# An attention and experts kernel: moving the splits off GpSimd and the second head's copies to ScalarE, with float64 words converted in blocks of 512

## The chip, the cores and the metric

The kernel runs on one core of a Trainium2 chip. The metric is the device time of one execution in microseconds. Before the change the median of three runs is 1041.32 us (1040.53 to 1044.79).

## What is computed

Attention over 4 batches, 8 heads, 576 positions and 64 values per head, with a bias that a small network makes of the distance of two positions; then a dense feed-forward (2304 tokens, 512 to 2048 to 512); then a routed one, in which each token goes to one of 8 experts. Cut to what matters:

```
scores = q @ k.T / sqrt(D) + bias
attn   = softmax(scores, axis=-1)
x = (attn @ v).reshape(2304, 512)
h = x @ w_in                          # w_in, w_out come as float64
x = maximum(0.01 * h, h) @ w_out
expert = argmax(normalised x @ normalised expert_emb / tau)
out[t] = gate[t] * (maximum(x[t] @ w1[expert], 0) @ w2[expert])
```

## The kernel before

**Splits.** The matmuls with weights and keys run on numbers in two parts: a high part (a rounded copy, type fp32r) and a low part (the exact value less the high part). So each operand that is split costs a copy (a line of the table `COPY`) and a subtraction (`LO`). Letters say which engine does them: P is GpSimd (POOL in the profile), A is ScalarE (ACT), D is VectorE (DVE). A string of four letters has one letter per batch, or for `WIN_*` one per four of the 16 column blocks of `w_in`. The helpers stand at L70 (ScalarE's copy), L74 (GpSimd's), L78 (VectorE's), L82 and L86 (the subtractions).

**float64 words.** `w_in` and `w_out` arrive as pairs of 32-bit words. `convert_f64` (L93) makes float32 of them with three VectorE operations (L99, L102, L105), of 256 elements per partition each. `w_in_split` (L120) loads half a column block of `w_in` (256 KB, L124), converts it and splits it into two resident tiles. `w_out_narrow` (L694) loads half a row block of `w_out` (L698), converts it and stores the float32 to DRAM (L703); it is read back only after attention. There are 32 of each. Raw words and results have two buffers each.

**Attention.** `phase1` (L559) walks 80 steps: 4 batches, in each two parts of the query rows (`hf`), four pairs of heads (`p`) and two or three blocks of rows (`ib`). A step has two heads, except where `ib` is 4: there both heads, 64 rows each, share one piece. In a step PE transposes the probabilities (L460, L482), the result is copied from PSUM to SBUF by the engine that `PROB_T` names (L464, L466), PE makes the scores two steps ahead (L409), VectorE adds the bias and takes the row's extreme (L414), ScalarE takes the exponential (L422), and `normalise` (L427) multiplies by the reciprocal sum, head by head, on the engine that `NORM` names. After a group PE multiplies by the values (L496). Between these pieces the program hands in 12-matmul pieces of `x @ w_in` for the groups that are done (`up_units`, L509); ScalarE, later ScalarE and then VectorE, empty their PSUM buffers (L527, L528, L530), of which there are two.

**What sets the order.** Side jobs (loads, splits, conversions) are put at a step and one of two positions in it (`put`, L577). The program is written in that order, but a scheduler then orders each engine's instructions by its own model, and may draw a job forward when its engine is idle there. On the chip each engine, and each queue of DMA issues, runs its list strictly in order. Nearly all loads are issued by the queue SP: the bias tiles of each step (L383 to L388), q, k, v, the raw words, and the stores of the converted words.

**After attention** come the rest of `x @ w_in`, the product with `w_out` (L769), and the experts (L1257, L1288). They hold little that the change touches.

Of the kernel before, what the change touches and what calls it, by code (L numbers as in the profile page):

```python
# [7 lines left out]
F32 = mybir.dt.float32  # L8
# [4 lines left out]
U32 = mybir.dt.uint32  # L13
# [34 lines left out]
NORM = ("PDDD", "PADD")  # L50
# [38 lines left out]
COPY = {"P": copy_pool, "A": copy_act, "D": copy_dve}  # L89
# [3 lines left out]
def convert_f64(nc, raw, t):  # L93


    w = raw.rearrange("p k (n two) -> p k n two", two=2)
    lo, hi = w[:, :, :, 0], w[:, :, :, 1]
    tu = t.bitcast(U32)
    nc.vector.tensor_scalar(  # L99
        out=tu, in0=hi, scalar1=3, scalar2=0x3FFFFFF8, op0=ALU.logical_shift_left, op1=ALU.bitwise_and  # L100
    )
    nc.vector.scalar_tensor_tensor(  # L102
        out=tu, in0=hi, scalar=0xC0000000, in1=tu, op0=ALU.bitwise_and, op1=ALU.bitwise_or
    )
    nc.vector.scalar_tensor_tensor(  # L105
        out=tu, in0=lo, scalar=29, in1=tu, op0=ALU.logical_shift_right, op1=ALU.bitwise_or
    )


def w_in_columns(e, f):  # L110

    c = 128 * (f % (KF // 2))
    return [w[:, :, c:c + 128] for w in e.wi[f // (KF // 2)]]
# [3 lines left out]
    return [p.tile([128, KD, FF // 2], F32R, name=f"wi{k}") for k in range(2)]  # L117


def w_in_split(nc, e, f, half):  # L120

    raw = e.cv.tile([128, 2, 256], U32, tag="w_raw", name="w_raw", bufs=2)
    src = e.w_in.rearrange("(k p) n -> p k n", p=128)
    nc.sync.dma_start(out=raw, in_=src[:, 2 * half:2 * half + 2, 256 * f:256 * f + 256])  # L124
    kc = slice(2 * half, 2 * half + 2)
    hi, lo = (w[:, kc] for w in w_in_columns(e, f))
    t = e.cv.tile([128, 2, 128], F32, tag="w_t", name="w_t", bufs=2)
    convert_f64(nc, raw, t)
# [155 lines left out]
class Attention:  # L284
# [142 lines left out]
    def normalise(self, st):  # L427
# [24 lines left out]
    def transposes(self, st, h):  # L452
        nc, e = self.nc, self.e
        b, hf, p, ib = st
        pr, _ = self.prob[st]
        ph, _ = self.pt
        o = 128 * (ib - HALVES[hf][2][0])
        ps = e.psT.tile([128, 512], F32, tag="t", name="pst")
        for c in range(4):
            nc.tensor.transpose(ps[:, 128 * c:128 * c + 128], pr[:, h, 64 * h + 128 * c:][:, :128], e.ident)  # L460
        if ib == 4:
            src = ps.rearrange("p (c h i) -> p h c i", c=4, h=2)
            for hh in range(2):
                COPY[PROB_T[b]](nc, ph[:, hh, :, o:o + 64], src[:, hh])  # L464
        else:
            COPY[PROB_T[b]](nc, ph[:, h, :, o:o + 128], ps.rearrange("p (c i) -> p c i", c=4))  # L466

    def transpose_tail(self, st):

        nc, e = self.nc, self.e  # L470
        b, hf, p, ib = st
        pr, _ = self.prob[st]
        pt = self.pt[1]
        o = 128 * (ib - HALVES[hf][2][0])
        ps = e.psT.tile([128, 512], F32, tag="t", name="psx")
# [83 lines left out]
def phase1(ctx, tc, e):  # L559

    nc = tc.nc
# [15 lines left out]
    def put(n, pos, f, *args):  # L577
        todo.setdefault((max(n, 0), pos), []).append((f, args))
# [5 lines left out]
    for k, g in enumerate(groups):  # L584
        b, hf, p = g
# [14 lines left out]
    for k in range(2 * KF):  # L600
        put(3 + k // 2 if k < KF else 12 + (k - KF) // 2, k % 2, w_in_split, nc, e, k // 2, k % 2)
    for k in range(2 * KF):
        put(20 + k, k % 2, w_out_narrow, nc, e, k // 2, k % 2)
# [750 lines left out]
def program(tc, e):  # L1354
# [4 lines left out]
    with ExitStack() as top:  # L1359
# [82 lines left out]
```

## Time and profile before

| | us |
|---|---|
| median of three runs | 1041.32 |
| the profiled execution, its own time | 1044.42 |
| its span in the trace | 1042.6 |
| PE busy | 991.1 (95%) |
| VectorE busy | 735.9 (71%) |
| ScalarE busy | 467.7 (45%) |
| GpSimd busy | 164.0 (16%) |

The span is the stretch from the first to the last instruction in the trace; some 1.8 us lie around it. Busy shares are means over the whole kernel, of which attention is the first half; what each engine does in a stage is read from a table by stretches. Ends of matmuls are modelled in this profile, so that PE busy is not PE at its peak; the weight loads (PEld) are a second reading of the same engine.

### The profile page before, as it was taken

What the parts mean: (1) busy time and instruction counts of PE and PEld (TensorE: products, weight loads), DVE (VectorE), ACT (ScalarE), POOL (GpSimd) and SP (SyncE); (2) the same over time, 40 slices, a digit from 0 to 9 for tenths busy, and PEclk for the clock granted to TensorE, in tenths of its full rate; (3) what the DMA queues carried; (4) which work ended last, traced back from release to release, by engine and by line L of the source; (5) the groups of instructions that cost most, each with busy time, mean ns of one, the idle gap of its engine ahead of it and who ended that gap; (6) DMA issues with size and microseconds to landing.
All of it is one profiled execution on the core that took longest, in us unless ns stands there. A gap on an engine that the chain in (4) does not pass through costs nothing.

```text
span 1042.6 us, 19336 instructions
## 1 busy us (share of the span) xinstructions
PE 991.1 (95%) x6294; PEld 809.0 (78%) x6294; DVE 735.9 (71%) x1907; ACT 467.7 (45%) x950; POOL 164.0 (16%) x204
## 2 busy tenths in 40 slices
PE   5999988999989999999999999999999999999995
PEld 2455777888778988898888888888877888888884
DVE  8878999888989899778866666769984256313312
ACT  5778665443333333333344333345462355424422
POOL 3233465000201011110000000001002111111210
PEclk9999999999999999999999999999999999999998
DMA  7877788877678576545357534336605158313410
GB/s 224 238 230 217 236 270 267 269 225 218 209 238 277 153 209 203 168 138 147 113 182 221 191 112 121 111 112 216 178 21 212 42 180 281 129 41 99 152 41 22
DMA packets 142466, 180.17 MB, mean 173 GB/s; under 512 B 20609, under 2 KB 94721, under 8 KB 142226
## 3 DMA queue, kind: packets, MB, share of 16 engines
q1 hardware_dynamic: 120418, 149.31, 47.0%
q10 hardware_dynamic: 18576, 19.03, 5.2%
q0 software_dynamic: 3360, 10.49, 3.0%
q8 instruction: 52, 0.85, 0.3%
q14 instruction: 60, 0.49, 0.2%
HBM read 196.18 MB, written 43.94 MB: 230 GB/s over the span
## 4 chain that ended last, share of the span: by engine, by line
PE 68%; DVE 16%; DMA 8%; issue 5%; ACT 1%; POOL 1%; SPq 0%; DVEq 0%; ACTq 0%; POOLq 0%
PE psx L769 19%; PE pu L1257 10%; PE pd L1288 10%; PE psh L521 9%; PE psv L496 5%; PE pss L409 4%; PE psb L266 4%; PE pst L460 4%; DMA wo_raw<-in_w_out_dram 3%; DVE prob L414 2%; DMA w_raw<-in_w_in_dram 2%; DVE kt L82 2%; DVE pth L78 2%; PE pt L1268 2%; DVE prob L438 1%
## 5 line engine op out<-in xcount | busy, mean ns | idle before, releaser
L521 PE MATMUL psh<-x,wi 128*128 128x256 f32 (+1 forms) x1536 | 229.5, 299 | 5.6 <-DVE hst L528 3.1
L521 PEld LDWEIGHTS psh<-x,wi 128*128 128x128 f32 x1536 | 212.5, 190 | 9.0 <-DVE hst L528 4.7
L422 ACT ACTIVATE prob<-prob,stat 128x576 f32<-128x576 f32 x144 | 111.6, 775 | 177.4 <-DVE stat L414 157.3
L769 PE MATMUL psx<-woh,gh 128*128 128x512 f32 x288 | 113.0, 392 | 0.1
L769 PE MATMUL psx<-wol,gh 128*128 128x512 f32 x288 | 112.7, 391 | 0.0
L769 PE MATMUL psx<-woh,gl 128*128 128x512 f32 x288 | 112.2, 390 | 0.0
L414 DVE CUSTOM_DVE_ANT_0 prob<-pss,prob 128x576 f32<-128x576 f32 x144 | 107.8, 750 | 4.4 <-PE pss L409 2.6
L460 PE MATMUL pst<-ident,prob 128*128 128x128 f32 x576 | 90.7, 279 | 9.1 <-DVE pth L78 4.0
L70 ACT ACTIVATE gh<-g 128x512 fp32r<-128x512 f32 x72 | 45.4, 632 | 115.7 <-PE psx L769 104.5
L460 PEld LDWEIGHTS pst<-ident,prob 128*128 128x128 f32 x576 | 66.0, 140 | 30.2 <-issue 12.0
L78 DVE COPY pth<-pst 128x512 f32<-128x512 f32 (+1 forms) x120 | 74.7, 632 | 12.2 <-PE pst L460 11.7
L409 PE MATMUL pss<-kt,qhi 128*128 128x288 f32 x256 | 81.2, 332 | 1.1 <-DVE stat L414 1.1
L496 PE MATMUL psv<-pth,vs 128*64 128x256 f32 (+1 forms) x512 | 73.3, 413 | 1.7 <-DVE pth L78 1.6
L266 PE MATMUL psb<-mk,cf 128*32 128x79 f32 (+47 forms) x640 | 61.0, 411 | 13.9 <-POOL cf L250 6.9
L409 PE MATMUL pss<-kt,qlo 128*128 128x288 f32 x256 | 72.7, 299 | 0.0
L1288 PE MATMUL pd<-w2h,hth 128*128 128x512 f32 x160 | 67.9, 424 | 4.1 <-ACTq L1213 4.1
L786 DVE SCALAR_TENSOR_TENSOR junk<-x1s,en 128x512 bf16<-128x512 f32 x96 | 66.1, 689 | 3.0 <-DMA en<-en_d 1.9
L82 DVE TENSOR_TENSOR htl<-pt,hth 128x512 fp32r<-128x512 f32 x40 | 27.1, 690 | 57.8 <-ACT hth L70 57.8
L82 DVE TENSOR_TENSOR gl<-g,gh 128x512 fp32r<-128x512 f32 x72 | 49.4, 689 | 23.6 <-ACT gh L70 19.3
L82 DVE TENSOR_TENSOR xl<-pt,xh 128x512 fp32r<-128x512 f32 x21 | 14.4, 690 | 72.4 <-ACT xh L70 72.4
L1257 PE MATMUL pu<-w1h,xh 128*128 128x512 f32 x160 | 65.1, 407 | 0.3 <-ACT xh L70 0.3
L1288 PE MATMUL pd<-w2h,htl 128*128 128x512 f32 x160 | 64.6, 404 | 0.0
(229 smaller groups left out, 1911.6 us busy)
## 6 DMA issues: line engine op xcount, KB each, us to landing
ws<-in_mw_dram SPq DMA_DIRECT2D x164, 512.0 KB
prob<-bias SPq DMA_DIRECT2D x64, 288.0 KB
g<-h SPq DMA_DIRECT2D x72, 256.0 KB
prob<-bias SPq DMA_DIRECT2D x64, 256.0 KB
bias<-bt SPq DMA_DIRECT2D x36, 295.5 KB
h<-hst ACTq DMA_DIRECT2D x64, 160.0 KB
w_raw<-in_w_in_dram SPq DMA_DIRECT2D x32, 256.0 KB
h<-hst ACTq DMA_DIRECT2D x64, 128.0 KB
```

What stands on the lines that cost most here:

```text
L78: nc.vector.tensor_copy(out, in_)
L82: nc.vector.tensor_tensor(out=out, in0=x, in1=hi.bitcast(F32), op=ALU.subtract)
L266: nc.tensor.matmul(ps[32 * q:32 * q + 32, :b - a], lhsT=cf[:, 4 * (m % COEF_M) + q], rhs=x, start=True, stop=True, tile_position=(0, 32 * q),)
L409: nc.tensor.matmul(ps[:, jh, :288], lhsT=lhsT, rhs=kt[:, c0 + 288 * jh:][:, :288], start=(k == 0), stop=(k == len(ops) - 1),)
L414: nc.vector.tensor_tensor_reduce(out=prv, in0=ps[:, :, :288], in1=prv, scale=-0.125, scalar=3.0e38, op0=ALU.add, op1=ALU.min, accum_out=st ...
L422: nc.scalar.activation(out=pr[:, h], in_=pr[:, h], func=AF.Exp, bias=stat[:, 0, h:h + 1], scale=-1.0, accum_out=stat[:, 1, h:h + 1],)
L460: nc.tensor.transpose(ps[:, 128 * c:128 * c + 128], pr[:, h, 64 * h + 128 * c:][:, :128], e.ident)
L496: nc.tensor.matmul(ps[64 * h:64 * h + 64, :n], lhsT=vs[:, c, h], rhs=ph[:, h, c, :n] if c < 4 else pt[:, :n], start=(c == 0), stop=(c == 4 ...
L521: nc.tensor.matmul(ps[:, :n], lhsT=w[:, kc], rhs=x[:, kc, :n], start=(k == 0), stop=(k == 3 * KD - 1),)
L769: nc.tensor.matmul(ps, lhsT=a[:, c % 4], rhs=w[:, c], start=(k == 0), stop=(k == 3 * KF - 1))
L1257: nc.tensor.matmul(ps, lhsT=a[:, k], rhs=w[:, k, c], start=(i == 0), stop=(i == 3 * KD - 1))
L1288: nc.tensor.matmul(ps, lhsT=a[:, k], rhs=w[:, k], start=(k == 0 and j == 0), stop=(k == 7 and j == 2))
```

## The change

The tables give GpSimd's splits to other engines: of `w_in` (high parts of the later half to ScalarE, the rest to VectorE), of q (high to ScalarE, low to VectorE), and keys of batches 2 and 3 go from VectorE to ScalarE. `NORM` for the second head in batches 2 and 3, and `PROB_T` for the second head in batches 1 to 3, go from VectorE to ScalarE. GpSimd keeps the key copies and the normalisations of batch 0, and the first small products of the bias. `convert_f64` works on 512 elements at a time, 16 blocks each of `w_in` and `w_out`, and the load, the three operations and the split of a block are handed in at successive half steps by the new `spread`.

```
-WIN_HI, WIN_LO = "DPPP", "DDPP"
-K_HI, K_LO = "PADD", "DDDD"
-Q_HI, Q_LO = "APPP", "DDPP"
-PROB_T = "ADDD"
+WIN_HI, WIN_LO = "DDAA", "DDDD"
+K_HI, K_LO = "PAAA", "DDDD"
+Q_HI, Q_LO = "AAAA", "DDDD"
+PROB_T = ("ADDD", "AAAA")
-NORM = ("PDDD", "PADD")
+NORM = ("PDDD", "PAAA")
...
-    raw = e.cv.tile([128, 2, 256], U32, tag="w_raw", name="w_raw", bufs=2)
+    raw = e.cv.tile([128, KD * 256], U32, tag="w_raw", name="w_raw", bufs=2)
...
+    yield
+    t = e.cv.tile([128, KD * 128], F32, tag="w_t", name="w_t", bufs=2)
+    yield from convert_f64(nc, raw, t)
...
-                COPY[PROB_T[b]](nc, ph[:, hh, :, o:o + 64], src[:, hh])
+                COPY[PROB_T[hh][b]](nc, ph[:, hh, :, o:o + 64], src[:, hh])
...
+    def spread_on(k, it, gap):
+        try:
+            next(it)
+        except StopIteration:
+            return
+        put((k + gap) // 2, (k + gap) % 2, spread_on, k + gap, it, gap)
+
+    for f in range(KF):
+        spread(2 + f if f < KF // 2 else 3 + f, 0, lambda f=f: w_in_split(nc, e, f), 1)
+    for c in range(KF):
+        spread(20 + 2 * c, 0, lambda c=c: w_out_narrow(nc, e, c), 1)
...
-    raw = e.cv.tile([128, 2, 256], U32, tag="w_raw", name="wo_raw", bufs=2)
+    raw = e.cv.tile([128, 2 * DM], U32, tag="w_raw", name="wo_raw", bufs=2)
     r = slice(128 * c, 128 * c + 128)
-    nc.sync.dma_start(
-        out=raw, in_=e.w_out[r, 512 * half:512 * half + 512].rearrange("p (k n) -> p k n", k=2)
-    )
+    nc.sync.dma_start(out=raw, in_=e.w_out[r])
```

**The order on VectorE.** The order of PE's matmuls against each other stays, but the conversions move on VectorE: of `w_out`, the last operation stood behind the 88th of the 144 score operations (L414, `ISA prob,stat`), and now stands behind the 64th (36 belong to each batch). All 16 blocks now lie in batch 1; the program text would put them in batches 1 and 2. From the 53rd score operation, before (`pst` is the transposes' PSUM buffer, `pth` where they are copied):

```order
L414 ISA prob,stat<-pss,prob 128x576
L414 ISA stat 128x1
L99 TENSOR_SCALAR wo_t<-wo_raw 128x256
L102 SCALAR_TENSOR_TENSOR wo_t<-wo_raw,wo_t 128x256
L99 TENSOR_SCALAR wo_t<-wo_raw 128x256
L105 SCALAR_TENSOR_TENSOR wo_t<-wo_raw,wo_t 128x256
L78 COPY pth<-pst 128x4x128
```

And now, from the same operation:

```order
L418 ISA prob,stat<-pss,prob 128x576
L418 ISA stat 128x1
L442 TENSOR_SCALAR prob<-prob,stat 128x576
L107 SCALAR_TENSOR_TENSOR wo_t<-wo_raw,wo_t 128x512
L99 TENSOR_SCALAR wo_t<-wo_raw 128x512
L418 ISA prob,stat<-pss,prob 128x576
L418 ISA stat 128x1
L103 SCALAR_TENSOR_TENSOR wo_t<-wo_raw,wo_t 128x512
```

A block now is as large as two before, and blocks follow each other about as closely as the halves did.

**The order on the queue SP.** The loads move with them: before, the 32 loads of `w_out` halves stood between the bias loads of steps 25 and 50; now 16 loads of 512 KB stand between those of steps 23 and 36. The loads around the bias tile of one step in batch 1 (`bias` is the DRAM tensor, `prob` the tile it is loaded to), before:

```order
L703 DMA wo<-wo_t 128x256 x2
L698 DMA wo_raw<-in_w_out_dram 128x512 x2
L385 DMA prob<-bias_63 128x576
L387 DMA prob<-bias_63 128x512
L388 DMA prob<-bias_63 128x64
```

And now, around the bias tile of a like step:

```order
L714 DMA wo_raw<-in_w_out_dram 128x1024
L389 DMA prob<-bias_63 128x576
L391 DMA prob<-bias_63 128x512
L392 DMA prob<-bias_63 128x64
L718 DMA wo<-wo_t 128x512
L714 DMA wo_raw<-in_w_out_dram 128x1024
L718 DMA wo<-wo_t 128x512
L714 DMA wo_raw<-in_w_out_dram 128x1024
```

A store (L718) waits for VectorE's last operation on its block, and the bias loads behind it wait with it.

**The order on ScalarE.** In batch 2, from the 93rd of the 144 exponentials, before:

```order
L422 ACTIVATE prob,stat<-prob,stat 128x576
L70 ACTIVATE hst<-psh 128x320
L531 DMA h<-hst 128x320
L70 ACTIVATE hst<-psh 128x256
L422 ACTIVATE prob,stat<-prob,stat 128x576
L531 DMA h<-hst 128x256
```

And now, where `kt` waits for a key load, `pth` for PE's transposes, and `hst` frees a PSUM buffer for PE:

```order
L426 ACTIVATE prob,stat<-prob,stat 128x576
L70 ACTIVATE kt<-kraw 64x576
L70 ACTIVATE hst<-psh 128x320
L535 DMA h<-hst 128x320
L426 ACTIVATE prob,stat<-prob,stat 128x576
L70 ACTIVATE hst<-psh 128x256
L70 ACTIVATE pth<-pst 128x4x128
L535 DMA h<-hst 128x256
L70 ACTIVATE qhi<-qraw 128x512
```

Behind each exponential there now stand two to four instructions where one or two stood.

## Rows read from the trace of the kernel before

**Rows 1.** Busy time by stretches: the start, late batch 0, batches 1, 2 and 3.
```profile
core 0: us, PE busy (x) PEld busy (x) DVE busy (x) ACT busy (x) POOL busy (x), PEclk, DMA share, GB/s
0.00:100.00 100.00, 85.92 (x792) 41.50 (x793) 84.98 (x214) 73.00 (x156) 31.41 (x47) 1.00 0.77 229
100.00:165.00 65.00, 58.15 (x454) 47.92 (x455) 58.27 (x161) 42.49 (x105) 36.79 (x51) 1.00 0.81 247
165.00:294.00 129.00, 117.94 (x877) 102.69 (x877) 112.72 (x317) 56.74 (x130) 17.65 (x28) 1.00 0.78 241
294.00:413.00 119.00, 116.47 (x883) 103.43 (x883) 107.31 (x290) 41.88 (x105) 17.56 (x20) 0.99 0.70 211
413.00:528.00 115.00, 115.00 (x894) 103.38 (x893) 94.98 (x267) 42.13 (x106) 13.03 (x16) 1.00 0.45 137
```

**Rows 2.** Exponentials of batch 1 by the same table; each counts twice, with its accumulator read.
```profile
165.00:294.00 129.00, 31.37 (x73) 1.00 0.78 241
```

**Rows 3.** The same table for the stretch after attention up to the experts.
```profile
575.00:780.00 205.00, 204.03 (x950) 167.65 (x948) 156.08 (x452) 85.36 (x151) 3.03 (x2) 1.00 0.44 134
```

**Rows 4.** VectorE by shape, batch 1: line, count, busy us, mean ns, idle before, releaser.
```profile
L78 DVE COPY pth<-pst 128x512 f32<-128x512 f32 x31 | 21.1, 684 | 1.0 <-PE pst L460 0.9
L438 DVE TENSOR_SCALAR prob<-prob,stat 128x576 f32<-128x576 f32 x20 | 10.6, 528 | 0.3
L102 DVE SCALAR_TENSOR_TENSOR wo_t<-wo_raw,wo_t 128x256 uint32<-128x256 uint32 x20 | 8.1, 420 | 0.1
L99 DVE TENSOR_SCALAR wo_t<-wo_raw 128x256 uint32<-128x256 uint32 x20 | 6.5, 330 | 7.7 <-DMA wo_raw<-in_w_out_dram 7.5
L82 DVE TENSOR_TENSOR qlo<-qraw,qhi 128x512 fp32r<-128x512 f32 x7 | 4.8, 687 | 3.6 <-POOL qhi L74 3.6
...
L78 DVE CAST kt<-kraw 64x576 fp32r<-64x576 f32 x7 | 3.2, 452 | 0.5 <-DMA kraw<-in_k_dram 0.4
...
L78 DVE COPY pth<-pst 128x256 f32<-128x256 f32 x6 | 2.3, 418 | 0.0
```

**Rows 5.** VectorE's waits in batch 3: us in total, times, longest.
```profile
DVE pth L78 <- PE pst L460: 7.7, 11, 1.0
DVE hst L528 <- ACT hst L527: 5.2, 9, 1.5
```

**Rows 6.** VectorE by shape, all of attention: the conversions and splits of `w_in`.
```profile
L102 DVE SCALAR_TENSOR_TENSOR w_t<-w_raw,w_t 128x256 uint32<-128x256 uint32 x32 | 16.3, 510 | 0.2
L105 DVE SCALAR_TENSOR_TENSOR w_t<-w_raw,w_t 128x256 uint32<-128x256 uint32 x32 | 16.0, 500 | 0.3
...
L99 DVE TENSOR_SCALAR w_t<-w_raw 128x256 uint32<-128x256 uint32 x32 | 12.1, 378 | 2.9 <-DMA w_raw<-in_w_in_dram 2.6
...
L82 DVE TENSOR_TENSOR wi<-w_t,wi 128x256 fp32r<-128x256 f32 x16 | 7.2, 448 | 1.0 <-POOL wi L74 0.8
...
L78 DVE CAST wi<-w_t 128x256 fp32r<-128x256 f32 x8 | 2.7, 336 | 0.0
```

**Rows 7.** The page's groups: a three-operand VectorE operation of 512 elements, after attention.
```profile
L786 DVE SCALAR_TENSOR_TENSOR junk<-x1s,en 128x512 bf16<-128x512 f32 x96 | 66.1, 689 | 3.0 <-DMA en<-en_d 1.9
```

**Rows 8.** VectorE by shape, 0 to 130 us: a one-operand operation of 512 elements.
```profile
L220 DVE TENSOR_SCALAR mk<-lw,v 128x512 f32<-128x512 f32 x5 | 3.0, 640 | 0.0
```

**Rows 9.** Busy time by stretches of 10 us, the columns of rows 1: where DMA is busiest.
```profile
195.00:205.00 10.00, 10.00 (x79) 9.21 (x79) 9.71 (x32) 6.90 (x15) 1.09 (x2) 1.00 0.90 287
325.00:335.00 10.00, 9.50 (x69) 7.88 (x68) 9.93 (x26) 2.94 (x9) 2.00 (x2) 1.00 0.95 289
```

**Rows 10.** ScalarE by shape, 60 to 330 us.
```profile
L70 ACT ACTIVATE pth<-pst 128x512 f32<-128x512 f32 x29 | 17.2, 592 | 9.1 <-PE pst L460 6.5 <-PE psv L496 1.6 <-ACT hst L70 0.5
...
L436 ACT ACTIVATE prob<-prob,stat 128x576 f32<-128x576 f32 x16 | 12.3, 770 | 6.5 <-DVE stat L432 6.5
...
L70 ACT ACTIVATE kt<-kraw 64x576 fp32r<-64x576 f32 x8 | 5.5, 682 | 2.1 <-DMA kraw<-in_k_dram 2.0
...
L70 ACT ACTIVATE qhi<-qraw 128x512 fp32r<-128x512 f32 x5 | 3.1, 625 | 0.0
```

More of the change, by code (lines that the diff above doesn't have):

```diff
@@ L93, in convert_f64 @@
 def convert_f64(nc, raw, t):
-    w = raw.rearrange("p k (n two) -> p k n two", two=2)
-    lo, hi = w[:, :, :, 0], w[:, :, :, 1]
+    w = raw.rearrange("p (n two) -> p n two", two=2)
+    lo, hi = w[:, :, 0], w[:, :, 1]
     tu = t.bitcast(U32)
@@ L104, in convert_f64 @@
     )
+    yield
     nc.vector.scalar_tensor_tensor(
@@ L117, in new_w_in, with w_in_split @@
     return [p.tile([128, KD, FF // 2], F32R, name=f"wi{k}") for k in range(2)]
-def w_in_split(nc, e, f, half):
-    raw = e.cv.tile([128, 2, 256], U32, tag="w_raw", name="w_raw", bufs=2)
+def w_in_split(nc, e, f):
+    raw = e.cv.tile([128, KD * 256], U32, tag="w_raw", name="w_raw", bufs=2)
     src = e.w_in.rearrange("(k p) n -> p k n", p=128)
[L124 to L128, printed above, removed]
+    nc.sync.dma_start(out=raw.rearrange("p (k n) -> p k n", k=KD), in_=src[:, :, 256 * f:256 * f + 256])
+    yield
+    t = e.cv.tile([128, KD * 128], F32, tag="w_t", name="w_t", bufs=2)
+    yield from convert_f64(nc, raw, t)
+    yield
+    hi, lo = w_in_columns(e, f)
+    t = t.rearrange("p (k n) -> p k n", k=KD)
     COPY[WIN_HI[f // 4]](nc, hi, t)
@@ L463, in transposes @@
             for hh in range(2):
-                COPY[PROB_T[b]](nc, ph[:, hh, :, o:o + 64], src[:, hh])
+                COPY[PROB_T[hh][b]](nc, ph[:, hh, :, o:o + 64], src[:, hh])
         else:
-            COPY[PROB_T[b]](nc, ph[:, h, :, o:o + 128], ps.rearrange("p (c i) -> p c i", c=4))
+            COPY[PROB_T[h][b]](nc, ph[:, h, :, o:o + 128], ps.rearrange("p (c i) -> p c i", c=4))
     def transpose_tail(self, st):
@@ L475, in transpose_tail @@
         ps = e.psT.tile([128, 512], F32, tag="t", name="psx")
-        copy = COPY[PROB_T[b]]
+        copy = COPY[PROB_T[0][b]]
         if ib == 4:
@@ L598, in phase1, with spread @@
             put(m + 3, 1, at.v_load, b, p)
[L600 to L603, printed above, removed]
+    def spread(n, pos, job, gap):
+        k = 2 * n + pos
+        put(k // 2, k % 2, lambda: spread_on(k, iter(job()), gap))
+    def spread_on(k, it, gap):
[8 more added lines that the diff above has]
+        spread(20 + 2 * c, 0, lambda c=c: w_out_narrow(nc, e, c), 1)
     bias_setup(nc, e)
@@ L691, in phase1, with w_out_narrow @@
     return fl
-def w_out_narrow(nc, e, c, half):
-    raw = e.cv.tile([128, 2, 256], U32, tag="w_raw", name="wo_raw", bufs=2)
+def w_out_narrow(nc, e, c):
+    raw = e.cv.tile([128, 2 * DM], U32, tag="w_raw", name="wo_raw", bufs=2)
     r = slice(128 * c, 128 * c + 128)
-    nc.sync.dma_start(
-        out=raw, in_=e.w_out[r, 512 * half:512 * half + 512].rearrange("p (k n) -> p k n", k=2)
-    )
-    t = e.cv.tile([128, 2, 128], F32, tag="w_t", name="wo_t", bufs=2)
-    convert_f64(nc, raw, t)
-    nc.sync.dma_start(out=e.wo_d[r, 256 * half:256 * half + 256], in_=t.rearrange("p k n -> p (k n)"))
+    nc.sync.dma_start(out=raw, in_=e.w_out[r])
+    yield
+    t = e.cv.tile([128, DM], F32, tag="w_t", name="wo_t", bufs=2)
+    yield from convert_f64(nc, raw, t)
+    nc.sync.dma_start(out=e.wo_d[r], in_=t)
 def w_out_units(nc, e):
```

## The prediction

> **What bounds the kernel now.** I read the table by stretches first, then each engine's instructions by shape, then the waits. Each batch of attention has 36 exponentials: the count in [rows 2], which has each twice, bears out that 165 to 294 us is batch 1, and the stretches beside it batches 2 and 3. The reader is to see in [rows 1] that the three batches hold the same PE work (103 us of weight loads in each), yet take 129, 119 and 115 us. What differs is VectorE: 112.7, 107.3 and 95.0 us busy. In batch 3 PE's row shows no gap in 115 us, and it is VectorE that waits for PE, 7.7 us for transposes [rows 5]. So **batch 3 goes at PE's pace, batches 1 and 2 at VectorE's**; late batch 0 also has VectorE at 58.3 of 65 us. DMA is the third: 0.78 to 0.81 of its engines' time in batches 0 and 1, 0.45 in batch 3. ScalarE has room: 56.7 of 129, 41.9 of 119, 42.1 of 115. Behind attention PE is full [rows 3] and the change touches nothing there that PE waits for; I count 0.
>
> **Batch 3: what leaves VectorE.** Second-head copies: 16 of 512 elements at 684 ns and 4 of 256 at 418 [rows 4], 12.6 us. Second-head normalisations: 16 at 528 ns, 8.5 us. Key copies: 8 at 452 ns, 3.6 us. What comes: 8 low parts of q at 687 ns, 5.5 us. Net 19.2 us off, 95 to 76. ScalarE gets [rows 10] 16 x 0.592, 4 x about 0.38 (my estimate, between the 592 ns of 512 elements and nothing), 16 x 0.770, 8 x 0.682 and 8 x 0.625 us: 33.8 us, 42 to 76 of 115. Since PE already sets the pace, I take 0.5 us of gain; the work that hides the rest is PE's own.
>
> **Batch 2.** The same 19.2 us, and the 12 halves of `w_out` that are converted here now (32 less 20 in [rows 4]) go to batch 1: each costs 0.330 + 2 x 0.420 = 1.17 us, 14 us together. VectorE 107.3 to 74. It then goes at PE's pace, as batch 3: 119 to 115.5, **3.5 us gained**. The cover that is lost is VectorE's own; late next is PE.
>
> **Batch 1.** Off: the copies, 12.6 us. The `w_out` work: 20 halves at 1.17 us, 23.4 us, become 16 blocks of 512 elements. A two-operand operation on those is priced by [rows 7], 689 ns. The one-operand one is not in the trace at 512 elements: between 0.33 [rows 4] and 0.64 us [rows 8], which reads a scalar beside; I take 0.43, nearer to the first, as the half has the same operands. A block is then 1.81 us, 16 are 29.0: 5.6 us more. By VectorE's new order the last three blocks of `w_in` fall here too: 3 x (1.81 + 0.69 for the low part) against some 6 halves at 1.39 now [rows 6], about 0. Net 7 us off: 112.7 to 105.7. VectorE's idle time, 16.3 us, loses the 3.6 us for GpSimd's high parts of q [rows 4], as ScalarE has room; the 7.5 us for `w_out` loads I leave, since the blocks follow as closely as the halves did. That makes 105.7 + 12.7 = 118.4 us by VectorE.
>
> But the loads that come forward must fit. DMA works 0.78 x 129 = 100.6 us here, at 241/0.78 = 309 GB/s. Twelve halves more, each 256 KB in and 128 KB out, are 4.7 MB, 15.3 us: 115.9 us of DMA work. The busiest ten microseconds show a share of 0.90 and 0.95 [rows 9]. At 0.95 batch 1 takes 122, at 0.90, 129. I take 123, near the first, since the new loads are large and prefetched by two blocks: **6 us gained**. The SP queue is the place: a store waits for VectorE, and the next bias tile waits behind the store.
>
> **Batch 0 and the start.** VectorE's `w_in` work: 32 x (0.378 + 0.510 + 0.500) = 44.4 us [rows 6] becomes 16 x 1.81 = 29.0, 15.4 us less. It takes on 8 low parts (5.5 us) and 4 high parts of GpSimd (1.7); larger pieces save 1.7 on the low parts it had (16 x 0.448 against 8 x 0.69) and 1.0 on the high ones (8 x 0.336 against 4 x 0.43). Net 10.9 us, of which 2 were counted in batch 1: 9 us off 143.3 busy in 165. The ends are 0, if DMA (0.81) or the bias's small products on GpSimd hold the pace, and 9, if VectorE does throughout. I take **4 us**, the middle, since late batch 0 has VectorE at 0.90 and DMA at 0.81.
>
> Two prices of one kind bear on this: with GpSimd busy 68 of 165 us, an operation that takes 420 ns on `w_out` takes 510 on `w_in` [rows 4, 6]. That is in the 44.4, and I count it gone.
>
> **The sum.** 4 + 6 + 3.5 + 0.5 = 14 us. The profiled execution took 1044.4 us, so 1030.4; the median of the runs lies 3.1 below it, so **1027.3 us** for the median after.
>
> **A rule against the change.** The rows give ScalarE 592 ns for a 512-element copy out of PSUM and VectorE 684, but for a normalisation from SBUF 770 against 528. The Trainium skill, in "ScalarE: Activation LUTs", section Rules for kernel authors, says to use VectorE and not ScalarE for multiplications and the like. By that rule the 32 normalisations of batches 2 and 3 lose 32 x 0.242 = 7.7 us of engine time, and were ScalarE the bound the sum would be 6.3 and not 14. The trace agrees on the price, but with ScalarE at 42 of 115 us the lost time lies beside PE's; and on the copies out of PSUM it says the opposite.
>
> **The rivals.**
>
> *PE is not full in batch 3.* The ends of matmuls are modelled, and weight loads fill 103.4 of 115 us, 0.90. If PE has gaps that VectorE's late copies cause, a relieved VectorE closes half of them: batches 2 and 3 go to 109 us, 10 and 6 gained in place of 3.5 and 0.5, the sum 26: **1015 us**. For it: VectorE is at 95 of 115 there, and copies of 0.68 us stand between PE's transposes and its products. Against: in the trace PE waits for nothing in batch 3. The skill's "Perfetto Trace Analysis", section Identifying the Most-Contended Engine, calls matmul busy time a bad measure and the weight loads' share a good one; by that rule this rival holds. The rows between agree in part: after attention weight loads show 167.7 of 205 us, 0.82, with PE without a gap [rows 3], so a share of 0.90 need not mean room. Chance 0.20.
>
> *The drawn-forward `w_out` loads eat the gain.* DMA in batch 1 holds no more than 0.88: 115.9 / 0.88 = 132 us, 3 lost; late batch 0 gains 3, not 4. Sum 3 - 3 + 3.5 + 0.5 = 4: **1037 us**, no change that shows. For it: `wo_raw` loads already stop VectorE for 7.5 us in batch 1, and a block takes longer to land than a half. Against: they are half as many, and steps 37 to 51 are free of them. Chance 0.18.
>
> *ScalarE's queue holds PE up: slower.* In batches 2 and 3 a normalisation waits for VectorE's reciprocal and a key copy for its load, and behind them in the same queue stand the instructions that empty PE's two PSUM buffers. If each of the 32 normalisations costs PE its whole 0.77 us, 24.6 us are lost: 14 - 24.6 = 10.6 us slower, **1052 us**. It decides from 14/32 = 0.44 us each. For it: in batch 3 VectorE already waits 5.2 us for ScalarE's part of emptying them [rows 5], and ScalarE goes from 42 to 76 us. Against: that is still two thirds, and the second head's turn comes half a step after the first's. Chance 0.14.
>
> **How the numbers follow.** The forecast has 0.48. A measurement of this kernel tells about 0.5%, 5.2 us, from no change. Faster by more: the forecast and the first rival, 0.68. Within it: the second, 0.18. Slower: the third, 0.14. The range takes in the bounds: below, 0 to 165 at its full 9, batch 1 at VectorE's 118.4 (10.6) and the first rival's 16 are 36 us together, 1006, which needs all at once; I stop at 1012. Above it reaches past the second rival to 1043, and leaves out most of the third.
>
> **What would show it.** Right: batch 2 at 114 to 117 us with VectorE near 75 and PE without gaps; batch 1 at 120 to 126 with DMA near 0.93; batch 3 at 114 or 115; no waits for GpSimd's q. Wrong: batch 3 under 112 (the first rival); `wo_raw` waits on VectorE above 15 us or batch 1 above 128 (the second); weight loads of PE waiting on `hst` or `pth` of ScalarE, batch 3 above 118 (the third); or a change in the stretch after attention, which I hold for untouched.

## The result, and the profile after

The changed kernel's median is **1028.76 us** (1027.66 to 1030.66, four runs), against 1041.46 (1040.53 to 1044.79, four runs) of the kernel before on the same chip: a ratio of 0.9881, with a 95% interval of 0.9855 to 0.9907. The forecast was 1027.3. The profiled execution took 1027.66 us, with a span of 1025.9; GpSimd's 61 us less and ScalarE's 80 more show on its page:

```profile
span 1025.9 us, 19107 instructions
PE 985.7 (96%) x6294; PEld 809.2 (79%) x6294; DVE 682.8 (67%) x1719; ACT 547.8 (53%) x1102; POOL 103.0 (10%) x112
```

The table by stretches of the changed kernel, with the columns of [rows 1]: late batch 0, batches 1, 2 and 3, and the stretch after attention.

```profile
107.00:161.00 54.00, 50.13 (x387) 42.30 (x386) 51.73 (x124) 41.16 (x103) 19.72 (x20) 1.00 0.91 283
162.00:281.00 119.00, 115.57 (x884) 103.23 (x883) 103.75 (x270) 74.87 (x168) 0.00 (x0) 1.00 0.87 281
281.00:395.00 114.00, 113.71 (x880) 101.85 (x879) 77.27 (x216) 73.36 (x162) 0.00 (x0) 1.00 0.59 178
395.00:510.00 115.00, 115.00 (x894) 103.37 (x893) 80.99 (x233) 67.36 (x153) 0.00 (x0) 1.00 0.46 139
...
556.00:761.00 205.00, 203.68 (x948) 167.34 (x946) 155.78 (x451) 85.14 (x151) 2.94 (x2) 1.00 0.43 134
```

Against [rows 1], batch 1 is 10 us shorter, batch 2 is 5 shorter and batch 3 as long as it was, and [rows 3] is matched to 0.4 us of PE. Such stretches are cut at round numbers. To compare kernels I cut at the starts of the score operations in the trace (144 on VectorE, 36 to a batch): the start up to the 19th, late batch 0 from there to the 37th, batch 1 to the 73rd, batch 2 to the 109th, batch 3 to the last; then the tail of attention, and the dense layers up to the experts. All tables below are cut so, in us, from the one execution of each kernel that was profiled; kernels that have a stage alike differ in it by 0.4 us in batches 2 and 3, by 1.2 in batch 1, and by up to 2.4 in the others.

| | start | late b0 | b1 | b2 | b3 | tail | dense | sum up to the experts |
|---|---|---|---|---|---|---|---|---|
| before | 105.8 | 57.8 | 129.4 | 119.7 | 108.7 | 32.1 | 219.5 | 773.1 |
| after | 107.0 | 54.0 | 119.1 | 114.3 | 109.1 | 31.1 | 219.6 | 754.2 |

So batch 0 gave 2.6 us, batch 1 10.3, batch 2 5.4 and batch 3 nothing. The experts, from there to the end, took 269.5 us before and 271.7 after, but 268.1 to 270.2 in the twelve kernels below. The two profiled spans lie 16.7 us apart, the medians 12.7: the profiled execution of before was 3 us above its median, that of after 1.1 below.

TensorE's clock also moves such stages. In every execution here the granted clock falls to the lower of its two levels (1.2 GHz, 0.50 in the column PEclk) for a few short stretches. Four of them, of before at the border of batches 1 and 2, of the blocks alone in the start, and of the four half buffers in batch 1 (two kernels described below):

```profile
292.80:296.20 3.40, 3.23 (x15) 3.23 (x16) 2.69 (x8) 0.87 (x2) 0.00 (x0) 0.51 0.67 215
...
48.80:52.20 3.40, 3.40 (x18) 1.28 (x16) 0.43 (x2) 1.44 (x3) 1.93 (x3) 0.50 0.93 301
...
210.90:214.30 3.40, 3.21 (x14) 3.21 (x15) 2.85 (x10) 2.37 (x6) 0.00 (x0) 0.50 0.91 281
255.30:258.70 3.40, 2.83 (x13) 2.83 (x14) 3.08 (x8) 1.63 (x3) 0.00 (x0) 0.50 0.53 182
```

At half the clock such a row of 3.40 us costs a stage 1.7 us at most, by my estimate. The start of the changed kernel took 106.7 to 107.1 us in five kernels that share it, and 108.4 and 108.5 in the two that had such a stretch near 48 us. So of batch 2's 5.4 us up to 1.6 are the stretch of before. Batch 0's 2.6 us are within the scatter: the seven kernels that have it as the changed one took 161.0 to 164.4 us for the start and late batch 0, against 163.6 before.

What VectorE waits for in batch 1 after (line waited for: us in total, times, longest):

```profile
DVE wo_t L99 <- DMA wo_raw<-in_w_out_dram: 7.7, 7, 2.1
DVE stat L435 <- ACT prob L426: 2.3, 4, 0.9
DVE qlo L82 <- ACT qhi L70: 1.7, 2, 1.0
```

The waits for `w_out` loads are those of [rows 4], 7.5 us, and GpSimd's 3.6 us became 1.7 for ScalarE. In batch 2 PE waits 0.3 us in all, and no wait of it is listed in batch 3:

```profile
PE psx L486 <- ACT pth L70: 0.3, 1, 0.3
```

### The profile page after: what moved, and what is told of

Same layout as the page of the kernel before. It is cut to its first block, busy times and chain, and to the rows that moved or that the text cites. A ratio compares the mean times of both kernels' runs of the same rounds, so it can differ in the third digit from the quotient of the medians.

```text
span 1025.9 us, 19107 instructions
## 1 busy us (share of the span) xinstructions
PE 985.7 (96%) x6294; PEld 809.2 (79%) x6294; DVE 682.8 (67%) x1719; ACT 547.8 (53%) x1102; POOL 103.0 (10%) x112
## 4 chain that ended last, share of the span: by engine, by line
PE 81%; DVE 7%; DMA 6%; issue 3%; ACT 1%; POOL 1%; SPq 0%; DVEq 0%; ACTq 0%; POOLq 0%
PE psx L784 19%; PE psh L525 15%; PE pu L1272 10%; PE pd L1303 9%; PE pss L413 7%; PE psv L500 7%; PE pst L464 5%; PE psb L270 3%; DMA wo_raw<-in_w_out_dram 3%; DVE mk L224 2%; PE pt L1283 1%; DMA w_t<-wo 1%; PE pt L1255 1%; DMA qraw<-in_q_dram 1%; PE psx L486 1%
## 5 line engine op out<-in xcount | busy, mean ns | idle before, releaser
L525 PE MATMUL psh<-x,wi 128*128 128x256 f32 (+1 forms) x1536 | 226.4, 297 | 1.4 <-DVE hst L532 1.3
L426 ACT ACTIVATE prob<-prob,stat 128x576 f32<-128x576 f32 x144 | 111.3, 773 | 66.2 <-DVE stat L418 58.7
L1241 POOL DMA_INDIRECT xg<-x,gidx x22 | 25.3, 1152 | 577.6 <-DMA ws<-in_mw_dram 549.1
L270 PE MATMUL psb<-mk,cf 128*32 128x79 f32 (+49 forms) x640 | 60.8, 420 | 13.9 <-POOL cf L254 6.8
L82 DVE TENSOR_TENSOR htl<-pt,hth 128x512 fp32r<-128x512 f32 x40 | 27.1, 689 | 57.8 <-ACT hth L70 57.8
L70 ACT ACTIVATE pth<-pst 128x512 f32<-128x512 f32 (+1 forms) x100 | 54.4, 548 | 20.6 <-PE pst L464 12.8
L1303 PE MATMUL pd<-w2l,hth 128*128 128x512 f32 x160 | 64.3, 402 | 0.0
```

The costliest lines, as they stand in the source:

```text
L70: nc.scalar.activation(out=out, in_=in_, func=AF.Copy)
L270: nc.tensor.matmul(ps[32 * q:32 * q + 32, :b - a], lhsT=cf[:, 4 * (m % COEF_M) + q], rhs=x, start=True, stop=True, tile_position=(0, 32 * q),)
L426: nc.scalar.activation(out=pr[:, h], in_=pr[:, h], func=AF.Exp, bias=stat[:, 0, h:h + 1], scale=-1.0, accum_out=stat[:, 1, h:h + 1],)
L525: nc.tensor.matmul(ps[:, :n], lhsT=w[:, kc], rhs=x[:, kc, :n], start=(k == 0), stop=(k == 3 * KD - 1),)
L1303: nc.tensor.matmul(ps, lhsT=a[:, k], rhs=w[:, k], start=(k == 0 and j == 0), stop=(k == 7 and j == 2))
```

## The experiments

**Each part alone.** The change has two parts, the tables and the blocks of 512. One kernel takes the tables and keeps the halves:

```diff
-WIN_HI, WIN_LO = "DPPP", "DDPP"
+WIN_HI, WIN_LO = "DDAA", "DDDD"
...
-PROB_T = "ADDD"
+PROB_T = ("ADDD", "AAAA")
-NORM = ("PDDD", "PADD")
+NORM = ("PDDD", "PAAA")
```

> The new tables alone; the float64 words stay in halves of 256 elements, handed in as before. Theory (VectorE's load set the pace of batches 0 to 2, and the tables and the larger blocks share the relief): the 10.9 us that the blocks save net on w_in and most of the 7.5 us on w_out (16 x 2 x 1.17 against 16 x 1.81 us) are back on VectorE, in batches 0 and 1, where it is near the bound; batches 2 and 3 as after the change (114 and 109 us from score operation to score operation). Time 1032 to 1037 us. Rival (the tables do it all, by taking GpSimd's contention away): 1028 to 1030. Rival (the blocks do it all): 1039 to 1042.

Measured: 1038.89 us (1035.15 to 1042.01, ten runs) against 1040.01, a ratio of 0.9989 (0.9968 to 1.0011): no difference, where 1032 to 1037 was expected. The other kernel is the opposite, with the tables of before:

```diff
-    for k in range(2 * KF):
-        put(20 + k, k % 2, w_out_narrow, nc, e, k // 2, k % 2)
+    for c in range(KF):
+        spread(20 + 2 * c, 0, lambda c=c: w_out_narrow(nc, e, c), 1)
```

> The blocks of 512 and the spread hand-in alone, with the tables of the kernel before. Theory: VectorE keeps the second head's copies (12.6 us a batch), so batch 1 stays near 126 us and batch 2 near 117, which only the departed w_out conversions help. Time 1034 to 1039 us. Rival (the blocks do it all): 1028 to 1031. Rival (the tables do it all): 1040 to 1042.

Measured: 1037.75 us (1033.96 to 1041.14, ten runs), 0.9981 (0.9959 to 1.0002), as small, and within the range expected. One after the other they would be worth 0.3%, together they are worth 1.2%. The stages:

| | start | late b0 | b1 | b2 | b3 | tail | dense |
|---|---|---|---|---|---|---|---|
| before | 105.8 | 57.8 | 129.4 | 119.7 | 108.7 | 32.1 | 219.5 |
| tables only | 105.8 | 57.3 | 126.9 | 116.9 | 109.1 | 33.4 | 220.6 |
| blocks only | 108.6 | 60.6 | 123.6 | 115.7 | 108.7 | 31.3 | 219.2 |
| both | 107.0 | 54.0 | 119.1 | 114.3 | 109.1 | 31.1 | 219.6 |

In batch 1 the gains nearly add: 2.5 (the tables' batch 1 holds a stretch at the lower clock, worth up to 1.7 us more) and 5.8 against 10.3. Most of the surplus is in batch 0: in these executions the blocks alone lose 5.6 us up to its end (2.8 in each column), and both parts together win 2.6. Some 1.6 us of that loss go with the stretch at 48.8 us, as in the starts above. The stretches late b0 and batch 1, first of the tables alone, then of the blocks alone:

```profile
105.80:163.10 57.30, 52.64 (x384) 42.38 (x383) 50.27 (x156) 38.59 (x100) 16.65 (x19) 1.00 0.83 257
163.10:290.00 126.90, 120.54 (x889) 104.81 (x889) 106.26 (x314) 80.45 (x181) 1.26 (x2) 0.99 0.82 248
```

```profile
108.60:169.20 60.60, 53.64 (x404) 44.24 (x403) 51.85 (x117) 39.25 (x100) 37.64 (x38) 1.00 0.79 248
169.20:292.80 123.60, 116.11 (x870) 101.63 (x869) 112.25 (x286) 53.57 (x125) 12.70 (x16) 1.00 0.85 275
```

With blocks alone VectorE is at 0.91 of batch 1, and GpSimd at 0.62 of late batch 0. PE's waits there show what GpSimd does to it: first before, then blocks alone, then after.

```profile
PE psx L482 <- POOL wi L86: 3.7, 2, 1.9
PE pst L460 <- POOL prob L440: 1.9, 3, 1.0
PE psx L482 <- POOL prob L440: 0.8, 2, 0.6
```

```profile
PE pst L464 <- POOL prob L444: 2.2, 5, 0.8
...
PE psx L486 <- POOL wi L86: 1.2, 2, 1.0
...
PE psx L486 <- POOL prob L444: 1.0, 1, 1.0
```

```profile
PE pst L464 <- POOL prob L444: 0.5, 1, 0.5
```

PE waited 6.4 us for GpSimd before and 4.4 with the blocks alone, and waits 0.5 now; all its listed waits there are 6.6, 6.9 and 3.8 us. GpSimd stands in PE's path with its normalisations of batch 0, which queue behind its subtractions; one of 512 elements holds its queue for 1447 ns:

```profile
L444 POOL TENSOR_SCALAR prob<-prob,stat 128x576 f32<-128x576 f32 x36 | 35.6, 1000 | 31.0 <-DVE stat L436 13.0 <-DMA prob<-bias 7.2 <-DMA h<-hst 3.6
...
L86 POOL TENSOR_TENSOR wi<-w_t,wi 128x512 fp32r<-128x512 f32 x8 | 11.6, 1447 | 0.3
```

What makes up the rest of the loss with blocks alone, and so most of the surplus, is not settled.

**What holds batch 3: PE or VectorE.** First, the second head's copies and normalisations of batch 3 go back to VectorE:

```diff
-PROB_T = ("ADDD", "AAAA")
+PROB_T = ("ADDD", "AAAD")
-NORM = ("PDDD", "PAAA")
+NORM = ("PDDD", "PAAD")
```

> The changed kernel with batch 3 alone undone: its second head's copies and normalisations go back to VectorE (21 us more there, 81 to about 102). Theory (PE sets the pace of batch 3 in both kernels): batch 3 stays at 108 to 110 us from its first to the last score operation, time within 1.5 us of the changed kernel's 1028.8. Rival (ScalarE's queue had taken VectorE's place as the bound there, so that nothing was gained): batch 3 at 106 or less, time 1025 to 1026. Rival (VectorE's relief does help batch 3): 3 us or more slower.

Second, PE is given less to do in batch 3: 32 pieces of `x @ w_in` leave out the product with the low part of `w_in`.

```diff
+            less = (b, hf) in ((2, 1), (3, 0))
-            for w, x in ((wh, xh), (wh, xl), (wl, xh)):
+            for w, x in ((wh, xh), (wh, xl), (wl, xh))[:2 if less else 3]:
```

> The changed kernel in which the 32 pieces of x @ w_in that lie in batch 3 leave out the product with the low part of w_in, 128 matmuls of about 0.13 us, 17 us of PE. Theory (PE sets the pace of batch 3): batch 3 goes from 109 to between 94 and 100 us. Rival (VectorE's and ScalarE's chain, not PE, sets it): 105 us or more.

Batch 3 of the two, the first above:

```profile
395.90:505.20 109.30, 109.22 (x842) 97.66 (x843) 91.75 (x256) 45.61 (x113) 0.00 (x0) 1.00 0.49 145
```

```profile
399.00:496.20 97.20, 97.20 (x732) 83.28 (x732) 76.10 (x222) 63.40 (x145) 0.00 (x0) 1.00 0.55 164
```

With 13 us more on VectorE batch 3 takes 109.3 us, as after (109.1); the time is 1028.27, 0.9870 (0.9845 to 0.9895) of before. With 113 matmuls fewer (732 in place of 845), some 17 us at 0.147 us each (226.4 us for 1536 of them on the page after), it takes 97.2, in a single run of 1018.55 us. PE's work moves batch 3 and the other two engines' doesn't. Twelve of the 17 us came back; why not all was not traced.

**What holds batch 1 now.** Here the suspects are VectorE and the drawn-forward loads. One kernel gives VectorE the second head's copies of batch 1 back:

```diff
-PROB_T = ("ADDD", "AAAA")
+PROB_T = ("ADDD", "ADAA")
```

> The changed kernel with the second head's copies of batch 1 alone back on VectorE (12.6 us; 103.8 to 116 of 119). Theory (VectorE's load set batch 1): batch 1 goes from 119 to 126 us or more, as its idle time for loads (8 us) stays; time 1034 to 1038 us. Rival (DMA or GpSimd's absence set it): batch 1 within 2 us of 119, time 1028 to 1031.

The other issues only two of the 16 `w_out` loads and converts those blocks again and again:

```diff
-    nc.sync.dma_start(out=raw, in_=e.w_out[r])
+    if c % 8 == 0:
+        e.wo_raw = e.cv.tile([128, 2 * DM], U32, tag="w_raw", name="wo_raw", bufs=2)
+        nc.sync.dma_start(out=e.wo_raw, in_=e.w_out[r])
+    raw = e.wo_raw
```

> The changed kernel in which only 2 of the 16 w_out blocks are loaded, each converted and stored 8 times: 7.3 MB less to load, VectorE's work unchanged; the output is that of a w_out made of two repeated blocks, so the routing differs and only the time up to the experts is compared. Theory (DMA, at 0.87 to 1.0, holds batch 1): batch 1 falls from 119 to 114 or 115 us, the waits for w_out blocks go. Rival (PE or VectorE holds it): batch 1 at 118 to 119.

Batch 1 of the two:

```profile
163.10:282.90 119.80, 116.87 (x885) 103.73 (x884) 110.05 (x283) 67.98 (x152) 0.73 (x1) 0.99 0.87 276
```

```profile
162.20:276.90 114.70, 114.21 (x884) 102.25 (x882) 103.23 (x270) 75.44 (x170) 0.74 (x1) 1.00 0.72 227
```

Fifteen more copies of 512 elements on VectorE (10.1 us by their durations, six of busy time, while its waits for loads fell from 7.7 to 5.3) cost 0.7 us, within the scatter (1027.72 us, 0.9859 of before, 0.9833 to 0.9885): the 126 us or more that were expected if VectorE's load set batch 1 did not come. Without 14 of the 16 loads batch 1 falls to 114.7 us, PE's pace, in a single run, with VectorE as busy as after. So the changed kernel's batch 1 is held by its loads. The chain of waits through batch 1 agrees. Its first line with the loads, then without them:

```profile
by line: DMA wo_raw<-in_w_out_dram 23.8%; PE psh L525 20.6%; PE pss L413 9.9%; PE psv L500 9.5%; PE pst L464 7.3%; DVE wo_t L103 3.9%; issue 3.6%; DVE wo_t L107 3.1%; DVE wo_t L99 2.4%; DVE prob L418 1.8%; DVE prob L442 1.6%; DVE pth L78 1.
```

```profile
by line: PE psh L525 42.9%; PE psv L500 18.0%; PE pss L413 17.8%; PE pst L464 13.2%; PE psx L486 2.2%; ACT kt L70 1.8%; issue 1.2%; ACT prob L426 1.1%; ACT pth L70 0.9%; ACT hst L70 0.6%; PE psx L482 0.5%; ACT qtail L70 0.2%; ACTq L426 0.0%
```

**Is it GpSimd's disturbance of VectorE?** The splits of q go back to the engines they had before, mostly GpSimd:

```diff
-Q_HI, Q_LO = "AAAA", "DDDD"
+Q_HI, Q_LO = "APPP", "DDPP"
```

> The changed kernel with q's high parts of batches 1 to 3 and low parts of batches 2 and 3 back on GpSimd (29 us of GpSimd work in attention). Theory (batches 2 and 3 go at PE's pace, batch 1 at DMA's): time within 2 us of the changed kernel, 1027 to 1031. Rival (GpSimd's absence frees VectorE of contention, and that is the gain): 1033 or more, with VectorE's operations longer by 5% or more in batches 2 and 3.

Measured: 1031.28 us (four runs), 0.9891 (0.9864 to 0.9918), an interval that overlaps that of the change; late b0, b1, b2 and b3 are 56.5, 121.9, 114.1 and 109.1. With GpSimd at 17 of 114 us in batch 2 that batch is as short as without it, though VectorE's normalisations take 568 ns there and 519 after. So the splits of q are a small share of the gain if any: the ratios lie 0.001 apart. What there is can be in batch 1, 2.8 us longer than after at full clock, where kernels alike differ by 1.2, and where VectorE waits 2.6 us for GpSimd's high parts of q:

```profile
164.80:286.70 121.90, 114.72 (x864) 101.69 (x863) 104.35 (x267) 70.16 (x156) 10.68 (x15) 1.00 0.86 270
```

**Spreading the loads.** If loads hold batch 1 and batch 2 has DMA free (0.59), the scheduler draws them forward too far. In three kernels a VectorE write into each raw buffer, which reads a probability tile of the step, keeps load c from running ahead of that step: every two steps, every three, and every two and a half with a third raw buffer.

```diff
-        spread(20 + 2 * c, 0, lambda c=c: w_out_narrow(nc, e, c), 1)
+        spread(21 + 3 * c, 0, lambda c=c: w_out_narrow(nc, e, c, at, steps[21 + 3 * c]), 1)
...
+    nc.vector.tensor_copy(raw[:, 0:1].bitcast(F32), at.prob[st][1][:, 0, 0:1])
     nc.sync.dma_start(out=raw, in_=e.w_out[r])
```

> The changed kernel, with each w_out load held back by a small VectorE write to its buffer that needs the row statistics of the step at which the program hands the block in (steps 20, 22, ... 50), so that the scheduler can't draw it forward: conversions end behind score operation 97 and not 64. Theory (batch 1 is now held by DMA at a share of 0.87 to 1.0, with 7.7 us of waits for w_out blocks): batch 1 falls from 119 to 115 or 116 us, batch 2 rises by no more than 1. Time 1025 to 1027 us. Rival (PE already holds batch 1): no change, 1028 to 1029. Rival (VectorE holds it, and takes the work later again): batch 2 up to 117, time 1029 to 1031.

> As e8_pin_2, but a block every three steps, steps 21 to 66, so that batch 3, which has DMA at 0.46, takes a part; conversions end behind score operation 124. Theory: batch 1 at 114 to 115 us, batches 2 and 3 as after the change or 1 us above; time 1024 to 1027 us. Rival (PE already holds batch 1): 1028 to 1030.

> e9_pin_3 with three raw buffers and a w_out block every two and a half steps, from 23 to 60. Theory (DMA no longer holds batch 1 and its load is evened out): batches 1 and 2 at 114 to 115.5 us each, time 1023 to 1026 us. Rival (what is left is PE): 1027 to 1029, as the changed kernel.

Measured:

| | us (runs) | ratio to before, 95% | profiled execution, us | b1 | b2 | DMA share in b1 |
|---|---|---|---|---|---|---|
| after | 1028.76 (4) | 0.9881 (0.9855 to 0.9907) | 1027.66 | 119.1 | 114.3 | 0.87 |
| every 2 steps | 1027.24 (4) | 0.9868 (0.9830 to 0.9906) | 1028.74 | 118.7 | 114.4 | 0.76 |
| every 3 steps | 1028.99 (5) | 0.9896 (0.9865 to 0.9927) | 1022.96 | 115.7 | 115.8 | 0.70 |
| every 2.5, 3 buffers | 1027.01 (5) | 0.9858 (0.9833 to 0.9884) | 1031.92 | 119.9 | 115.5 | 0.71 |

The stages of "every 3 steps" are what the theory wants, 3.4 us less in batch 1 for 1.5 more in batch 2, but they are those of the fastest of its five runs (those of "every 2.5" of the slowest), and its time, like the others', is not told apart from the changed kernel's: no better version came out. All three medians lie above what was expected, and batch 1 fell as expected in none, though nearly so with "every 3 steps". "Every 2 steps" and "every 2.5" show that the mean DMA share is not what decides. With 0.71 the VectorE of "every 2.5" waits for loads more than after, though a pinned load need not cost that (3.9 and 2.9 us in the other two); what does was not traced:

```profile
DVE wo_t L99 <- DMA wo_raw<-in_w_out_dram: 11.1, 6, 3.3
```

**Is it bytes in flight?** Two buffers of 512 KB hold twice as much in flight as two of 256 KB. So the tables alone and the kernel before get four half buffers in place of two:

```diff
-    raw = e.cv.tile([128, 2, 256], U32, tag="w_raw", name="wo_raw", bufs=2)
+    raw = e.cv.tile([128, 2, 256], U32, tag="w_raw", name="wo_raw", bufs=4)
```

> e1_tables_only with four buffers of 256 elements instead of two, for raw words and results: as many bytes in flight as the changed kernel has with two of 512. Theory (with the tables, batch 1 is held by the loop of loading a half, converting it and freeing its buffer; the block's size matters by the bytes in flight): batch 1 falls from 127 to 119 to 121 us, batch 2 to 115; time 1029 to 1032 us. Rival (it is the 48 instructions fewer on VectorE, or the larger descriptors): batch 1 stays at 125 or more, time 1037 to 1039.

> The kernel before with four such buffers and nothing else changed. Theory (VectorE at 113 us and the loop of loads together make batch 1's 129 us; buffers take the second away): batch 1 at 123 to 125 us, as in e2_blocks_only; batch 2 at 116 to 118; time 1035 to 1038 us. Rival (VectorE alone): batch 1 at 128 or more, time 1040 to 1042.

Measured: with the tables 1035.66 us (seven runs) against 1042.50, 0.9937 (0.9917 to 0.9958), about half of the change's gain; without them 1043.78 (ten runs), 1.0010 (0.9989 to 1.0031), nothing. Expected were 1029 to 1032 and 1035 to 1038. Batch 1, for which the edit was made, was missed too: 129.0 and 126.8 us. Batch 1 of the first, and its wait:

```profile
162.80:291.80 129.00, 117.67 (x875) 104.90 (x875) 107.78 (x331) 76.64 (x174) 1.55 (x1) 0.97 0.85 264
```

```profile
DVE wo_t L99 <- DMA wo_raw<-in_w_out_dram: 12.7, 8, 3.4
```

The buffers draw all 32 halves into batch 1, as the blocks are drawn, and there the bytes are about those of the change (264 GB/s x 129.0 us = 34.1 MB; 281 x 119.1 = 33.5 MB). They take 0.85 x 129.0 = 110 us of DMA work in place of 104, and VectorE waits 12.7 us in place of 7.7. Two stretches at the lower clock are in this batch 1 (PEclk 0.97 in its row); without them it would take 125.6 us at the least. What this execution gains is mostly batch 2's, 114.3 us with the conversions gone from it, but it is the slowest of the seven, 5.4 us above their median, and where the median run gains the rest was not traced. So as far as this execution shows, bytes in flight do not replace the blocks. In the other kernel, batches 1 and 2 win 6.2 us, and the start and late batch 0 (60.9) lose 5.9; in each of the two sums up to 1.7 us are the clock.

## Why the prediction was right, and where it was not

**Batch 2** ended as argued: VectorE fell from 107.3 to 77.3 us (74 forecast), PE waits 0.3 us, and the batch lost 5.4 us, up to 1.6 of them by the clock, where 3.5 were forecast; it ended at 114, PE's pace, rather than 115.5. That VectorE had set its pace is argued from PE's waits before, 294 to 413 us, all of them for VectorE:

```profile
PE psh L521 <- DVE x L82: 0.8, 1, 0.8
PE pst L460 <- DVE pth L78: 0.6, 1, 0.6
PE psx L482 <- DVE pth L78: 0.5, 1, 0.5
PE psv L496 <- DVE pth L78: 0.5, 1, 0.5
```

They are 2.4 us, less than the gain, and no run gives VectorE its work back in batch 2 alone. In the other kernels that take work off VectorE there, the batch takes 114.1 to 116.9 us with VectorE anywhere from 74 to 96 us, and not in that order.

**Batch 3** went as argued too: no gain, since PE was full, which the two experiments on it show directly. One term under it was mis-sized: VectorE was to fall by 19 us and fell by 14 (95.0 to 81.0). The key copies of that batch, 3.6 us, lie in batch 2's stretch, and 6 low parts of q came in place of 8. The instructions that left and came make 13.4 + 9.1 + 0.4 - 4.1 = 18.8 us by count and mean duration (copies, normalisations, one sum of `hst`, low parts of q), near the forecast, and busy time still fell by only 14. The durations of all VectorE instructions in this batch add up to 111.3 us before and 92.6 after, where busy time is 95.0 and 81.0: neighbours overlap in the records, so what leaves the busy time was three quarters of the sum of durations. Nothing hung on it here, as PE set the pace.

**Batch 1** is the step that failed in its size: 6 us forecast, 10.3 measured, and 119.1 us (up to 120.3 in two kernels that have it alike) where 123 were forecast. VectorE came out as argued (103.8 us busy for 105.7, the waits for loads kept at 7.7). The DMA term was too dear. I had 115.9 us of DMA work at 309 GB/s, and a stage that holds no more than 0.95. It was 0.87 x 119.1 = 104 us: 33.5 MB, 2.3 more than before (241 x 129.4 = 31.2) where I had added 4.7, at 281 / 0.87 = 323 GB/s. The kernels with halves move 309 (before), 302 (tables only) and 311 GB/s (four buffers) for a full share, the one with blocks only 324. Longer rows explain little of that: a packet of 4096 bytes, a row of a block, takes 189 ns in batch 1 after, one of 2048 took 98 ns before, but the bias rows of 2304 bytes also went from 135 to 127 ns. Why the rate rose stays open. Batch 2 lost what I counted (211 x 119 less 178 x 114 is 4.8 MB); of the half that isn't in batch 1, late batch 0 has 0.7 MB (283 x 54.0 less 253 x 57.8), and the rest was not followed. Nor is 0.95 a top:

```profile
162.00:172.00 10.00, 10.00 (x81) 8.37 (x80) 8.94 (x23) 9.04 (x22) 0.00 (x0) 1.00 0.97 318
...
182.00:192.00 10.00, 10.00 (x78) 9.22 (x75) 8.57 (x22) 4.35 (x11) 0.00 (x0) 1.00 1.01 353
```

What I had right of it is which resource holds the stage after the change: the loads, not VectorE, as the kernel with two loads shows. That they hold it by the DMA engines' share of time, as my term had it, is not shown: pinned loads gave 118.7 us at 0.76 and 119.9 at 0.71. Of VectorE's relief, the copies were my largest item, 12.6 us, and taking them back costs 0.7 us; taking back the splits of q costs 2.8, and the blocks alone win 5.8, each read from one execution.

**Batch 0** gave 2.6 us where I took 4, and the scatter of 3.4 us between kernels alike does not tell the two apart. I counted as gone what GpSimd's work costs VectorE there. It is not: GpSimd still works 55 us up to the end of batch 0, and the same operations on `w_in` stay dearer than on `w_out`. VectorE by shape, 0 to 281 us after:

```profile
L103 DVE SCALAR_TENSOR_TENSOR wo_t<-wo_raw,wo_t 128x512 uint32<-128x512 uint32 x16 | 11.1, 691 | 0.2
L99 DVE TENSOR_SCALAR wo_t<-wo_raw 128x512 uint32<-128x512 uint32 x16 | 6.8, 424 | 7.8 <-DMA wo_raw<-in_w_out_dram 7.7
L103 DVE SCALAR_TENSOR_TENSOR w_t<-w_raw,w_t 128x512 uint32<-128x512 uint32 x16 | 12.3, 771 | 0.1
L107 DVE SCALAR_TENSOR_TENSOR w_t<-w_raw,w_t 128x512 uint32<-128x512 uint32 x16 | 11.8, 737 | 0.0
L99 DVE TENSOR_SCALAR w_t<-w_raw 128x512 uint32<-128x512 uint32 x16 | 7.3, 458 | 0.4 <-DMA w_raw<-in_w_in_dram 0.3
L82 DVE TENSOR_TENSOR wi<-w_t,wi 128x512 fp32r<-128x512 f32 x16 | 12.6, 794 | 0.4 <-ACT wi L70 0.4
```

On `w_out` the block costs 0.424 + 2 x 0.691 = 1.81 us, to the digit what I estimated from [rows 7] and a choice between [rows 4] and [rows 8]. On `w_in` it costs 1.97, and its low part 0.794 in place of 0.69; over 16 blocks that is 4.2 us of the 9 that I had as the upper end. What I also did not see is PE's waits for GpSimd, 6.4 us in late batch 0 and 0.5 now; that they are a part of the gain no run shows by itself.

**The rivals.** *PE is not full* fell: batch 3 is no shorter after, and no longer with VectorE loaded again. The Trainium skill, "Perfetto Trace Analysis", section Identifying the Most-Contended Engine, judges TensorE's headroom by MFU (the share of the peak arithmetic rate that is used) and the share of weight loads. Read as room on PE, the 0.90 of weight loads does not fit the trace here: the batch follows PE's work down by 12 us. *The drawn-forward loads eat the gain* named the right resource and too high a price; the waits stayed at 7.7 us, and batch 1 at 119.1, below its 132. *ScalarE's queue holds PE up* fell: PE waits 0.3 us for ScalarE in batch 2 and none is listed in batch 3, and giving the work of batch 3 back to VectorE changes nothing. The normalisations cost ScalarE 773 ns as [rows 10] said, and that lies beside PE's work.

**The sum** was 14 us as 4 + 6 + 3.5 + 0.5; the stages give 2.6 + 10.3 + 5.4 - 0.4 = 17.9 in two executions whose spans differ by 16.7, and the medians differ by 12.7. The total is nearer than its terms, and in part by luck: batch 1 was taken 4 us too low, and the medians lie 4 us nearer to each other than the profiled executions. The prediction allowed for the 3 us by which the profiled execution of before was above its median; that of after was 1.1 below its own, and its experts took 2.2 us longer. Of batches 0 and 2 the errors, 1.4 too high and 1.9 too low, are no larger than what scatter and clock make.

## What to carry to other kernels

Find for each stage what ends last, and give work away only there. Then ask what the engine that is relieved will run earlier: here it drew the loads of one stage into another, and the loads became that stage's limit. Two edits of one change can be worth next to nothing apart and their worth together, so a part that moves nothing alone is not thereby useless. Before reading a gain from two traces, see how far each lies from its median and where its clock fell. Before subtracting durations from an engine's busy time, add up the stage's groups and see whether they exceed it.

## What the runs showed of the hardware that I had not expected

- DMA engines can be busy at a share of 0.97 to 1.01 over ten us (318 to 353 GB/s), with the stage still moving at PE's pace (PE 10.00 of 10.00 us in both rows above).
- Nearly the same bytes cost more DMA work as halves: 110 us at 34.1 MB (halves, four buffers) against 104 at 33.5 MB (blocks), and 12.7 against 7.7 us of waits. The rows' length, the number of issues (32 or 16) and the number of VectorE instructions behind them change together, and no run here separates them.
- With the tables of before, late batch 0 did not become shorter with four buffers, 60.9 us for 57.8 (up to 1.7 of it the clock, 0.97 there), nor with blocks (60.6): more loads in flight did not help there. Both have GpSimd's splits of `w_in` (36 and 38 us of GpSimd); with the tables of the change, four buffers give 53.7. That GpSimd's queue is the cause is argued from PE's waits, not shown by an edit of `WIN_HI` and `WIN_LO` alone.
- A stretch of 3.4 us at the lower TensorE clock cost the start of the changed kernel some 1.6 us near 48 us, and 0.4 at most at 16 to 23 us. VectorE is nearly idle in the first (0.43 of 3.40 us with blocks alone) and busy in the second (3.30 of 3.40 after); that this makes the difference is not shown.
